# Loads of q, k and v on two queues, and a new order table, in a fused attention and maxout kernel

## The chip, the cores and the metric

The kernel runs on one core of a Trainium2 chip. The metric is the device time of one execution in microseconds (us). The kernel before has a median of 292.42 us over three timed runs (290.92 to 293.25).

## The reference

There are 64 heads (8 batches of 8), each with 576 tokens of 64 features, and a linear attention with exponential features, followed by a feed-forward layer with a maximum over three products:

```python
def phi(x):
    proj = np.einsum('bhsd,df->bhsf', x, w_phi)                # 64 -> 128
    proj = proj - np.max(np.abs(proj), axis=-1, keepdims=True)
    return np.concatenate([np.exp(proj), np.exp(-proj)], axis=-1)
q_p, k_p = phi(q), phi(k)
kv = np.einsum('bhsf,bhsd->bhfd', k_p, v);  z = np.sum(k_p, axis=2)
num = np.einsum('bhsf,bhfd->bhsd', q_p, kv)
den = np.einsum('bhsf,bhf->bhs', q_p, z)[..., None] + 1e-06
x = (num / den).transpose(0, 2, 1, 3).reshape(4608, 512)
h = np.maximum(np.maximum(x @ w1, x @ w2), x @ w3)             # 512 -> 768
return h @ w_out                                               # 768 -> 512
```

Inputs and output are float32. The kernel rounds to bfloat16 for its products.

## The kernel before

The work is cut into 16 units of four heads each, two units to a batch, and nine chunks of 512 tokens for the feed-forward layer. The Python code does not issue instructions where it describes them. It makes nodes: each node is a step on one engine, with the function that issues its instructions, the steps it depends on, and the buffers it touches. A table, `PLAN`, written out as text, then says in which order all 1479 nodes are issued, on which engine each one runs, and which slot of its pool each buffer takes. A word such as `1081G@5.1` is node 1081 on GpSimd (`G`; `D` VectorE, `A` ScalarE, `T` TensorE, `S` Sync) at a planned 5.1 us; digits behind the letter are the slots. Each engine executes its own words strictly in that order, and so do the queues from which DMAs are issued. The planned times only sort the words and, on TensorE, tell `fill` where fill products (`idler`) go in: products with no use that keep TensorE active in gaps of the first part.

A unit goes through these steps. The letters are the names of the node kinds, and the numbers are those of the units (K0 is the step K of unit 0).

- Loads of q, k and v. Units 0 to 3 have q and k transposed by TensorE, the others by a DMA transpose. Unit 0's q and k come in halves through Sync in float32 and are cast on chip (step C); those of units 1 to 3 come through GpSimd's queue, which casts to bfloat16 on the way. From unit 4 on, q and k come through Sync in float32 and GpSimd casts them. All v loads come through Sync. A one-element copy (gate) holds some v loads back.
- T, the transposition into qkT, and Tc, the copy out of PSUM.
- G, the products with w_phi (psq, psk); r, the maxima on VectorE; ek, the exponentials of k on ScalarE.
- E, the exponentials of the maxima (em), and va, the products of v with em into vab. These run on GpSimd. vd copies em beside them.
- M and eq, the features of q with their maxima taken off.
- K, the products of features and v: 72 small matmuls into kvps at L633, which need vab of the unit. kv copies them out.
- N and x, the numerator and the division; X, the transposition of the result into xT.

The weights w1, w2, w3 and w_out come through GpSimd's queue in four loads (W0, W1, W2 and wout), with a cast. The kernel uses max(a, b, c) = a + max(0, b - a, c - a): the differences w2 - w1 and w3 - w1 are formed on chip in three parts each (step wd, L775), the first three on GpSimd and the others on VectorE, and w1 is folded into w_out. For that, w1 is transposed on TensorE (wt at L787, into pwT, which needs W0) and multiplied with w_out (wm at L801, which needs wout). A chunk then is `up` and `up2` (L704), which need the differences, and `down` (L732, L737).

Of the kernel before, what the change touches and what calls it, by code (L numbers as in the profile page):

```python
# [19 lines left out]
P = 128  # L20
# [28 lines left out]
VA_DVE = 1  # L49
# [50 lines left out]
56A@14.3 35D@13.4 50A0@14.8 65A@15.0 104T111211@13.5 66T5@13.8 158G2@3.4 68A@15.5 108D@14.0 30D@14.6 46A@15.8 88T6@14.1  # L100
89D@15.2 92T7@14.9 93D@15.8 107D@16.0 60T3@15.3 61A@16.1 94T46@16.0 98D@16.6 105A@16.6 67A@17.1 99T71@16.8 102D@17.2
96A@17.4 62A@17.9 97D@17.9 101A@18.4 157G@4.2 163T5@17.6 164D2@18.5 1081G@5.1 1091T7@18.1 1092D0@19.1 109T34@18.7 112D@20.2
161T0@19.0 1084G@5.9 106A@18.9 110A@19.4 95A@19.9 1095T5@19.6 1096A@20.3 114T2@20.0 117D@20.8 116A@21.3 103D@21.2 162D@21.8
111A@21.7 1093T7@20.4 52G0@15.2 47G@16.3 115A@22.1 53G@17.4 49G@17.7 51G@18.0 48G@19.1 69T063@21.0 71A@22.5 133T51@22.1
134A@22.9 70A@23.4 130T0@22.6 159D2@22.4 113D@22.5 118D@23.1 1094D@23.5 100A@23.8 135A@24.3 230G0@20.2 1082G@21.0 229G@21.8
74T30@23.0 75D0@24.6 1083G@22.7 119A1@24.8 122G1@25.1 132A@25.0 78T4@23.4 127T2@23.7 136T6@24.1 137A@25.5 72T1@24.6
73D1@25.2 79D0@25.8 182T007500@25.0 185D@26.5 184A@26.0 138A@26.5 123A@26.9 186D@27.1 1099T3@25.4 1100D@27.7 1101T1@26.7
1102D@28.3 131A@27.2 129A@27.7 177T46@28.1 87S@7.4 120G@25.4 121G@26.5 172T70@28.3 175D@28.9 76T3@28.6 183A@28.2 128A@28.7
165T5@28.9 166D@29.5 178A@29.1 173A@29.6 179A@30.1 139T1@29.1 174A@30.6 1103T2@29.3 140A@31.1 1104A@31.4 180D@29.7 77D1@30.3
181D@31.0 187T7@30.6 191D@31.6 126G@27.7 125G@27.9 124G@29.1 142T154@30.9 176D@31.9 144A@32.1 141A@32.5 143A@32.9 367S1@17.2  # L110
370G1@30.2 167T36@31.9 171D@32.5 195A0@33.3 169A@33.5 189A@34.0 198A0@34.4 188A@34.5 1085G@31.3 235T2@32.3 236D0@33.1
170D@33.7 82T0@32.9 80T4@33.1 81A@34.9 145T11@33.4 146D0@34.3 147T5@33.8 148D1@35.0 190D@35.6 1097T2@34.1 168A@35.5 83A@36.0
1098A@36.6 149T3@35.4 150D0@35.9 151T1@35.7 152D1@36.5 233T4@36.0 234D@37.2 254T115711@36.6 256A@37.1 237T6@37.0 238D@37.8
257D@38.0 153T3@37.1 192T0@37.4 193A0@37.7 231D3@38.6 154A@37.9 155T2@37.5 156A@38.6 255A@39.2 160S@22.6 197G@33.7
244T14@37.9 247D@38.7 196G@35.8 214T006@38.2 216A@39.7 215D@39.4 245A@40.1 249T35@39.2 250A@40.6 252D@39.8 239T21@39.5
242D@40.4 240A@41.1 251A@41.6 258D@41.0 1090D@41.6 241A@42.1 1107T0@39.9 366S1@27.2 259T6@40.8 263D@42.2 1087G@37.9
1115T3@41.0 1116A1@42.5 1108A@43.0 261A@43.5 246A@43.9 1109T2@41.9 253D@42.5 369G@40.0 1088D@43.1 1117T7@42.7 1118A@44.4
302S0@32.6 305G2@41.1 194S@38.1 199T30@43.6 211T5@43.8 212A@44.9 213A@45.4 200A@45.7 243D@43.8 262D@44.4 248D@44.7
1129T0@43.9 1130D@45.3 1086G@42.2 1111T1@44.8 208T7@45.6 1112D@45.9 1110D@46.5 209A@46.2 267A1@46.7 264T4@45.9 265A1@46.9
1127T5@45.9 1128D@47.1 1113T0@46.8 202T1@47.7 432S1@38.8 435G0@44.3 232S@39.4 268G1@47.1 260A@47.2 210A@47.5 201A@48.0  # L120
1114A@48.5 205T2@47.9 207A@49.0 371S1@41.2 203A@49.5 204A@50.1 1089D@47.8 206A@50.6 372T004600@48.2 376D@48.6 387T57@48.4
389A@51.1 390D@49.2 375D@49.8 1119T3@48.7 1120D@50.4 301S0@44.1 1125T0@49.6 1126D@51.1 373A@51.6 270G@49.2 1121T5@50.5
388A@52.1 377T41@51.4 380D@51.9 1122D@52.5 382T32@51.7 385D@53.1 374A@52.5 1123T0@52.0 1124D@53.7 378A@53.0 1135T4@52.8
219T60@53.7 392T5@54.0 384A@53.5 379A@54.0 394A@54.5 266S@47.3 368S1@48.0 277T31@54.2 278A@54.8 692S0@48.6 431S1@49.3
283T0@54.5 285A@55.3 383A@55.7 304G@49.6 562S1@49.9 306S2@50.8 561S0@55.9 393A@56.2 284A@56.5 1136T@54.6 1137A0@56.8
1138S@57.6 220D0@54.3 381D@54.9 391D@55.5 386D@56.3 217T6@55.9 218D1@56.9 274T1@56.2 275A@57.4 395D@57.5 396D@58.0 276A@58.1
400A0@58.6 279A@58.8 1131T7@56.4 221T0@57.3 222D0@58.4 269G@50.7 286T124@57.7 288D@59.0 280T6@58.8 281A@59.3 223T5@59.0
397T1@59.3 398D0@59.6 287D@59.8 271T0@59.4 273A@59.8 282A@60.3 272A@60.8 402G0@59.0 434G@61.1 564G1@62.2 565G@63.3
225T3@59.6 226D@60.2 224D1@60.6 1132T@59.9 1133A1@61.4 312T114111@61.3 315D@61.7 307T23@61.5 322T65@61.8 323A@62.2 325D@62.3
293T01@62.1 294D0@62.9 310D@63.6 314A@62.7 324A@63.2 313A@63.7 316D@64.3 1139T7@62.4 326D@64.9 227T4@63.3 228D@65.5  # L130
399S@59.9 404T60@63.5 406A@64.1 309A@64.6 405A@65.1 1140T@63.8 327T0@65.1 328A@65.6 563S0@60.6 407T2@65.3 410T1@65.5
412A@65.9 1141A2@66.4 409A@67.0 311D@66.0 330D@66.6 295T5@65.7 411A@67.5 408A@68.0 331D@67.1 296D1@67.4 291T6@66.0
292D0@68.0 1143T4@66.3 289T7@67.2 290D1@68.6 436S0@62.3 303S2@65.2 496S1@65.8 329A@68.5 498S3@66.5 1144T@67.5 1145D3@69.3
308A@68.8 416T1@68.8 418A@69.3 413T5@68.9 415A@69.7 299T2@69.1 300A@70.2 297T6@69.4 298D@69.9 417A@70.8 317T07@69.8
320D@70.4 321D@71.0 695G2@64.4 403G@65.5 401G@65.8 419T034@70.0 421D@71.6 499G0@71.6 332T6@71.2 333D1@72.0 334S@72.3
335A1@71.7 338G1@72.7 337G@73.0 420D@72.2 1155T2@71.2 1167T0@72.1 1156D0@72.6 1168D@73.3 319A@72.0 414A@72.5 318A@73.0
447T001400@73.1 449A@73.5 452T63@73.3 455D@73.9 453A@74.0 437T52@73.5 439A@74.5 448A@75.0 438A@75.5 454A@75.9 440D@74.5
450D@75.1 441D@76.1 1157T7@73.9 1158A@76.4 1165T0@74.7 457T6@75.6 459A@76.9 428T50@75.8 429D0@76.7 566S1@73.0 628S1@75.9
451D@77.3 461D@77.9 1153T1@76.1 1154A@77.3 1166D@78.3 1149T2@77.0 442T75@77.9 443A@78.4 445D@78.9 1150A@78.9 458A@79.4
444A@79.7 336G@75.1 354T114@78.2 356A@80.2 355D@79.5 424T0@79.3 348T21@79.6 349A@80.6 460D@79.9 425D1@80.2 350A@81.2  # L140
# [145 lines left out]
def kernel(  # L286
# [133 lines left out]
    def attention(u):  # L420
# [4 lines left out]
        def nd(kind, *args, **kw):  # L425
            return node(kind, u, *args, **kw)
# [437 lines left out]
```

## Time and profile before

| what | value |
|---|---|
| timed runs | 290.92, 292.42, 293.25 us |
| span of the profiled execution (its own time; the profile gives no other for it) | 290.5 us |
| median of the runs less that span | 1.92 us |
| TensorE busy | 276.3 us (95%) |
| VectorE, ScalarE, GpSimd busy | 213.8, 193.8, 116.9 us |
| read from HBM, written to it | 34.67 MB, 9.44 MB |

The profile is of one execution. Its page gives, for each engine, the time in which it was busy, and the same in 40 equal slices as digits (9 is 90% or more). The engines are called PE (TensorE; PEld are its weight loads), DVE (VectorE), ACT (ScalarE), POOL (GpSimd) and SP (Sync); a q behind the name is the engine's issuing queue. PEclk is the clock that TensorE was granted, in tenths of full speed. The chain is the path of work that ended last, followed back from the end. In rows of a group, the numbers behind the first bar are the busy time in us and the mean of one in ns; behind the second bar stands how long the engine was idle ahead of them, and what ended that. In a timeline, a row begins with its start and length in us; brackets hold the idle time ahead and its releaser. For DMA issues, the last number is the time from issue to landing in us.

### The profile page before, as it was taken

The page shows a single profiled execution, that of the slowest core. Times are in us where ns is not written, and L with a number is a line of the kernel's source. Part 1 is how long each engine was busy: PE and PEld are TensorE (multiplying, and loading weights), DVE is VectorE, ACT ScalarE, POOL GpSimd, SP SyncE. Part 2 cuts the span into 40 slices and gives each one's busy share as a digit, 9 for nine tenths or more (in the row PEclk, how much of TensorE's full clock was granted, in tenths as well). Part 3 has the DMA queues.
Part 4 walks back from the last instruction along what each step waited for, and adds up shares of the span by engine and source line. Part 5 has one row for each costly group of instructions (what it writes and reads, how often), then busy time and mean ns, then how long its engine had stood idle before and what let it go on. Part 6 is the DMA issues. An engine that isn't in the chain of part 4 may idle for free.

```text
span 290.5 us, 8509 instructions
## 1 busy us (share of the span) xinstructions
PE 276.3 (95%) x3518; PEld 157.4 (54%) x3555; DVE 213.8 (74%) x449; ACT 193.8 (67%) x446; POOL 116.9 (40%) x99
## 2 busy tenths in 40 slices
PE   8678999899999999999999999999999999999995
PEld 3447676356656655555555566555544654444443
DVE  5695899998998967988979879878963382455411
ACT  1795989789898989976797898858758510021021
POOL 8055789728373662817180753500077001000000
PEclk9997999999999999999999999999999999999999
DMA  7999967899999999997999545982240109414045
GB/s 184 280 242 199 246 198 181 197 360 212 231 241 361 150 257 253 275 262 157 225 324 273 118 83 156 164 167 45 52 115 2 39 10 208 91 39 95 12 122 170
DMA packets 65649, 50.83 MB, mean 175 GB/s; under 512 B 46154, under 2 KB 50378, under 8 KB 65610
## 3 DMA queue, kind: packets, MB, share of 16 engines
q1 hardware_dynamic: 61279, 45.03, 63.2%
q0 software_dynamic: 4000, 4.92, 9.9%
q8 instruction: 28, 0.46, 0.6%
q10 hardware_dynamic: 331, 0.33, 0.3%
q14 instruction: 11, 0.09, 0.1%
HBM read 34.67 MB, written 9.44 MB: 152 GB/s over the span
## 4 chain that ended last, share of the span: by engine, by line
PE 66%; DMA 13%; DVE 10%; POOL 5%; issue 2%; SPq 2%; ACT 2%; ACTq 0%; POOLq 0%; DVEq 0%
PE ups L704 22%; PE ops L737 13%; PE ops L732 9%; DMA w_bf<-in_moe_w_dram 6%; PE psn L651 5%; DMA qkT<-qk_bf 5%; PE kvps L633 5%; PE psm L604 3%; PE psq L525 3%; DVE mk L544 3%; DVE hT L710 2%; POOL vab L579 2%; DMA q_raw<-in_q_dram 2%; DVE mqp L544 2%; PE pm L801 2%
## 5 line engine op out<-in xcount | busy, mean ns | idle before, releaser
L704 PE MATMUL ups<-xT,w_bf 128*128 128x512 bf16 x412 | 101.7, 379 | 2.5 <-DVE mk L544 0.9
L617 ACT ACTIVATE Eq<-psm 128x512 bf16<-128x512 f32 (+1 forms) x160 | 82.3, 584 | 9.6 <-PE psm L604 8.2
L579 POOL TENSOR_TENSOR vab<-v_raw,em 128x1152 bf16<-128x1152 f32 (+1 forms) x36 | 67.9, 1904 | 44.6 <-ACT em L575 31.7
L538 ACT ACTIVATE Ek<-psk 128x512 bf16<-128x512 f32 x128 | 70.6, 616 | 8.3 <-PE psk L525 5.1
L704 PEld LDWEIGHTS <-w_bf 128*128 128x128 bf16 x432 | 40.6, 98 | 47.2 <-issue 2.3
L544 DVE TENSOR_REDUCE mqp<-psq 128x4 bf16<-128x512 f32 (+1 forms) x80 | 48.8, 632 | 8.3 <-PE psk L525 4.9
L737 PE MATMUL ops<-wout_bf,hT 128*128 128x512 bf16 (+1 forms) x215 | 50.4, 373 | 0.4
L710 DVE TENSOR_TENSOR hT<-hT,ups 128x512 bf16<-128x512 bf16 x54 | 35.9, 681 | 12.3 <-PE ups L704 8.5
L544 DVE TENSOR_REDUCE mk<-psk 128x4 f32<-128x512 f32 x64 | 42.6, 682 | 1.8 <-PE psk L525 1.1
L745 ACT COPY osb<-ops 128x512 f32<-128x512 f32 (+1 forms) x18 | 10.5, 590 | 38.2 <-PE ops L737 35.7
L737 PEld LDWEIGHTS <-hT 128*128 128x128 bf16 x222 | 21.0, 98 | 22.3
L658 DVE TENSOR_TENSOR x_sb<-psn,rden 128x320 bf16<-128x320 f32 x64 | 31.5, 491 | 2.2
L712 ACT ACTIVATE hT<-ups 128x512 bf16<-128x512 f32 x32 | 19.8, 627 | 17.2 <-PE ups L704 17.2
L651 PEld LDWEIGHTS <-Eq 128*128 128x128 bf16 x640 | 25.2, 97 | 7.7
L651 PE MATMUL psn<-kv_sb,Eq 128*128 128x65 bf16 x640 | 27.3, 194 | 0.0
L745 DVE COPY osb<-ops 128x512 f32<-128x512 f32 (+1 forms) x19 | 12.8, 673 | 19.5 <-PE ops L737 16.4
L732 PE MATMUL ops<-xT 128*128 128x512 bf16 x89 | 24.0, 380 | 0.4
L525 PE MATMUL psq<-w,qkT 64*128 64x128 bf16 x256 | 21.5, 219 | 0.8 <-DMA qkT<-qk_bf 0.8
L604 PE MATMUL psm<-qkT,wphi_m 128*128 128x512 bf16 (+1 forms) x70 | 22.3, 358 | 0.0
L525 PE MATMUL psk<-w,qkT 64*128 64x128 bf16 x256 | 21.4, 219 | 0.0
L714 DVE TENSOR_SCALAR hT<-ups 128x512 bf16<-128x512 f32 x22 | 14.8, 685 | 8.4 <-PE ups L704 8.4
L633 PE MATMUL kvps<-vab,Ek 64*128 64x65 bf16 x1152 | 20.1, 190 | 0.4 <-POOL vab L579 0.4
(76 smaller groups left out, 266.7 us busy)
## 6 DMA issues: line engine op xcount, KB each, us to landing
v_raw<-in_v_dram SPq DMA_DIRECT2D x16, 576.0 KB, 5.4
out_dram<-osb SPq DMA_DIRECT2D x66, 128.0 KB, 2.4
k_raw<-in_k_dram SPq DMA_DIRECT2D x12, 576.0 KB, 4.5
q_raw<-in_q_dram SPq DMA_DIRECT2D x12, 576.0 KB, 6.0
w_bf<-in_moe_w_dram POOLq DMA_DIRECT2D x3, 768.0 KB, 17.0
qk_bf<-in_q_dram POOLq DMA_DIRECT2D x3, 288.0 KB, 10.9
qk_bf<-in_k_dram POOLq DMA_DIRECT2D x3, 288.0 KB, 10.7
wout_bf<-in_moe_w_out_dram POOLq DMA_DIRECT2D x1, 768.0 KB, 21.0
```

Source lines behind the costliest of these rows:

```text
L525: nc.tensor.matmul(ps()[:, i, :], lhsT=cols[r, :], rhs=w2[r, c, :], start=True, stop=True)
L538: nc.scalar.activation(Ek[s]()[:, tiles_of(t0, n), :], of(1), EXP, scale=1.0 - 2.0 * s)
L544: nc.vector.tensor_reduce((mq, mk)[c]()[:, tiles_of(t0, n)], of(c), AXX, ALU.max, apply_absolute_value=True)
L579: (nc.vector if n_.eng == "DVE" else nc.gpsimd).tensor_tensor(vab()[:, g, t0:t1, 0:D], vb()[:, t0:t1, :], em()[:, g, t0:t1].unsqueeze(2).t ...
L617: nc.scalar.activation(Eqb()[s][:, cols], psm()[:, 0:w], EXP, scale=1.0 - 2.0 * s)
L633: nc.tensor.matmul(kvps[ab]()[:, t // NT, g, :], lhsT=Ek[g]()[r, t, :], rhs=vab()[r, g, t, :], start=(t + g == 0), stop=(t == UT - 1 and g ...
L651: nc.tensor.matmul(psn()[:, c, :], lhsT=Eqb()[g][:, t0:t0 + P], rhs=kv()[:, pr, ab, g, :], start=(g == 0), stop=(g == 1))
L658: nc.vector.tensor_tensor(x_sb()[:, pr, :, ab, :], psn()[:, :, 0:D], rden().to_broadcast([P, 5, D]), ALU.mult)
L704: nc.tensor.matmul(ups(), lhsT=w_bf[i + 1][:, ct, j * P:(j + 1) * P], rhs=tokens_of(ct), start=(ct == 0), stop=(ct == CT - 1))
L710: nc.vector.tensor_tensor(hT()[:, j, :], hT()[:, j, :], ups(), ALU.max)
L732: nc.tensor.matmul(ops_()[:, 0:width], lhsT=tile_of(ct, tt), rhs=line_w[c_i > MOVE][:, ct, cols], start=(ct == 0), stop=False)
L737: nc.tensor.matmul(ops_()[:, 0:width], lhsT=hT()[:, j, tt * P:(tt + 1) * P], rhs=wout_bf[:, j, cols], start=False, stop=(j == JT - 1))
```

## The change

- `VA_DVE` goes. The products of v may run on VectorE for unit 0, at a new planned cost; the table still has them all on GpSimd.
- q, k and v loads in float32 (all but unit 0's q and k) may be issued by Sync or by GpSimd. The table puts 12 q and k loads and 3 v loads on GpSimd: v of units 0, 2 and 9, and q or k of units 4, 5, 7, 8, 10, 11, 12, 13, 14 and 15. Sync keeps the others.
- Unit 0's q and k lie side by side in qk_bf, so that one 128-column transpose turns both, where a 64-column transpose each did. That is 18 transposes instead of 36. The casts into qk_bf run on ScalarE, all four; two of them were on VectorE.
- All six weight differences run on GpSimd. Three were on VectorE.
- `PLAN` is another table: order, engines, slots and planned times. The DMA order on GpSimd becomes k1, q1, W0, k2, q2, v0, wout, W1, k5, q5, k3, q3, v2, W2, k4 and so on; it was q1, k1, k2, q2, W0, wout, k3, W1, q3, W2. Sync starts with q0, k0, k0, q0 in halves, and then v1. Six kv copies and two copies out of wm go from VectorE to ScalarE, six of the chunks' rectifications from ScalarE to VectorE, three stores from Sync to ScalarE. There are 26 fill products instead of 23. The amount of other TensorE work is the same.

```diff
-VA_DVE = 1
 ...
 PLAN = (another table)
 ...
-    queue_of = {"SP": nc.sync, "ACT": nc.scalar}
+    queue_of = {"SP": nc.sync, "ACT": nc.scalar, "POOL": nc.gpsimd}
 ...
-        qk = buf("qk_bf", QK, [P, 2, UT, D] if by_pe else [P, UT, 2 * D], BF16)
+        qk = buf("qk_bf", QK, [P, 2, UT, D] if by_pe and u else [P, UT, 2 * D], BF16)
 ...
-                            copy_on[n_.eng](qk()[:, what, ts, :], raw()[:, ts, :])
+                            copy_on[n_.eng](qk()[:, ts, what * D:(what + 1) * D], raw()[:, ts, :])
 ...
-                mains.append(nd("Lv" if what == 2 else "L", {"SP": 0.62}, lambda what=what, raw=raw: nc.sync.dma_start(
-                    by_pairs(raw()), rows_of(what, u, 0, 2)), gates, [raw],
 ...
+                n_ = nd("Lv" if what == 2 else "L", {"SP": 0.62, "POOL": 0.75}, None, gates, [raw],
 ...
+                n_.fn = lambda n_=n_, what=what, raw=raw: queue_of[n_.eng].dma_start(by_pairs(raw()), rows_of(what, u, 0, 2))
+                mains.append(n_)
 ...
+                        if u == 0:
+                            nc.tensor.transpose(tps()[:, n, :], qk()[:, t, :], ident)
+                            continue
                         for c in range(2):
                             nc.tensor.transpose(tps()[c * D:(c + 1) * D, n, :], qk()[:, c, t, :], ident)
 ...
-                if VA_DVE > u:
-                    costs["DVE"] = 0.11 + 0.105 * (t1 - t0)
+                if u == 0:
+                    costs["DVE"] = 0.11 + 0.064 * (t1 - t0)
 ...
-            n_ = node("wd", 0, {"DVE": 0.6} if i else {"POOL": 2.1}, None, [w_nodes[0], w_nodes[i + 1]], [])
+            n_ = node("wd", 0, {"DVE": 1.2, "POOL": 2.1}, None, [w_nodes[0], w_nodes[i + 1]], [])
```

More of the change, by code (lines that the diff above doesn't have):

```diff
@@ L100 @@
[L100 to L109, printed above, removed]
@@ L462, in attention @@
                         raw()[0:1, 0, 0:1], src()[0:1, col:col + 1]), [], [src, raw]))
-                mains.append(nd("Lv" if what == 2 else "L", {"SP": 0.62}, lambda what=what, raw=raw: nc.sync.dma_start(
-                    by_pairs(raw()), rows_of(what, u, 0, 2)), gates, [raw],
-                    pipe=(EARLY if u == 0 or u == BY_PE and what == 1 else 1.0) * FULL, hold=-3.0, lat=1.7,
-                    packet=PACKET))
+                n_ = nd("Lv" if what == 2 else "L", {"SP": 0.62, "POOL": 0.75}, None, gates, [raw],
+                        pipe=(EARLY if u == 0 or u == BY_PE and what == 1 else 1.0) * FULL, hold=-3.0, lat=1.7,
+                        packet=PACKET)
+                n_.fn = lambda n_=n_, what=what, raw=raw: queue_of[n_.eng].dma_start(by_pairs(raw()), rows_of(what, u, 0, 2))
+                mains.append(n_)
         for c in range(0 if by_pe else 2):
```

280 lines of the change are left out of this document (148 added, 132 removed).

## The prediction

> **What bounds the kernel now.** I read the page first: the span, the busy shares, the slices and the chain.
>
> ```profile
> span 290.5 us, 8509 instructions
> PE 276.3 (95%) x3518; PEld 157.4 (54%) x3555; DVE 213.8 (74%) x449; ACT 193.8 (67%) x446; POOL 116.9 (40%) x99
> ...
> PE   8678999899999999999999999999999999999995
> ...
> PEclk9997999999999999999999999999999999999999
> DMA  7999967899999999997999545982240109414045
> ...
> PE 66%; DMA 13%; DVE 10%; POOL 5%; issue 2%; SPq 2%; ACT 2%; ACTq 0%; POOLq 0%; DVEq 0%
> ```
>
> TensorE is busy in nine tenths of every slice but the first four and the last, and carries two thirds of the chain. Only the first 29 us, where PE has holes and one slice of reduced clock, have much to give. So I cut the span at PE's landmarks: its longest hole, the first key-value product (unit 0's kvps, K0), and the fifth (unit 5's, K5).
>
> ```profile
> core 0: us, PE busy (x) PEld busy (x) DVE busy (x) ACT busy (x) POOL busy (x), PEclk, DMA share, GB/s
> 20.54:22.98 2.44, 0.00 (x1) 0.00 (x1) 1.03 (x2) 1.34 (x3) 2.44 (x3) 0.96 1.22 207
> 22.98:27.01 4.03, 4.03 (x50) 3.34 (x51) 1.64 (x3) 1.64 (x3) 2.45 (x4) 0.60 1.19 195
> 27.01:78.04 51.03, 49.42 (x828) 31.26 (x835) 48.09 (x103) 46.48 (x113) 35.12 (x26) 1.00 0.93 229
> 78.04:290.50 212.46, 206.02 (x2440) 113.97 (x2464) 148.72 (x307) 131.60 (x302) 68.24 (x50) 1.00 0.66 155
> ```
>
> PE stands for 2.44 us, then works 4.03 us at a clock of 0.60. From K0 on it idles 1.61 us in 51.03, and 6.44 us in the last 212.46. The timeline tells who ended the hole, and the chain in order of time what was on the path:
>
> ```profile
> 22.98 1.03 PE L787 MATMUL pwT<-ident,w_bf 128*128 128x128 bf16 x8 [2.44 <-DMA w_bf<-in_moe_w_dram]
> 27.01 1.27 PE L633 MATMUL kvps<-vab,Ek 64*128 64x65 bf16 x72
> 78.04 1.26 PE L633 MATMUL kvps<-vab,Ek 64*128 64x65 bf16 x72
> ```
> ```profile
> 4.96 17.97 DMA w_bf<-in_moe_w_dram
> ...
> 48.04 0.88 DVE w_bf L775
> ...
> 49.85 1.53 DVE w_bf L775
> ...
> 55.37 1.56 DVE w_bf L775
> ...
> 287.07 0.37 ACT osb L745
> ```
>
> W0 (the first maxout weight) is issued at 4.96 and lands at 22.93; its transposes on PE wait for it with everything behind them. Later, three weight differences on VectorE (3.97 us) lie on the chain.
>
> **The change, part by part.** *The waypoint.* In the two orders the same PE instructions stand ahead of K5, apart from fill products and unit 0's transposes, and so the same ones behind it. Ahead of K0 the new order has everything that the old one has, and four transposes of unit 2 and three M groups of unit 1 more. So the gain is K0's shift, plus the work that is now ahead of K0, plus what changes in the holes after K0.
>
> *GpSimd's DMA queue.* Old: q1, k1, k2, q2, W0, wout. New: k1, q1, W0, k2, q2, v0, wout, W1, k5, q5, k3, q3 (a letter and its unit). W0 moves past two loads, and v0 comes from Sync to sixth place here. The rates, from the old queue:
>
> ```profile
> 2.82 1.46 POOL L452 DMA_DIRECT2D qk_bf<-in_k_dram  x2
> ...
> 4.25 0.75 POOL L452 DMA_DIRECT2D qk_bf<-in_q_dram  x1
> ...
> 5.71 0.88 POOL L413 DMA_DIRECT2D wout_bf<-in_moe_w_out_dram  x1
> ...
> 9.60 0.67 ACT L445 CAST qk_bf<-q_raw 128x576 bf16<-128x576 f32 x1 [1.08 <-DMA q_raw<-in_q_dram]
> ...
> 22.44 0.77 POOL L452 DMA_DIRECT2D qk_bf<-in_k_dram  x1
> ```
> ```profile
> DMA to landing us min/median/max: 5.8/10.8/14.9
> ```
> ```profile
> qk_bf<-in_k_dram POOLq DMA_DIRECT2D x3, 288.0 KB, 10.7
> wout_bf<-in_moe_w_out_dram POOLq DMA_DIRECT2D x1, 768.0 KB, 21.0
> ```
>
> The middle answer is that of the qk_bf tile. k1, issued at 2.82, landed 10.7 us later, at 13.5; q2 (4.25 + 14.9) at 19.2; W0 at 22.9; wout (5.71 + 21.0) at 26.7; k3 (22.44 + 5.8) at 28.2. So a weight takes 3.8 us of the queue, a q or k load 1.5 us when no Sync load runs beside it, and 2.8 us each ((19.2 - 13.5) / 2) with Sync loads beside it. In the new order Sync has its four halves in by 9.6, as now, and then only v1, which waits behind some ten VectorE instructions for a gate that comes at about 16 (estimate). From 9.6: k1 needs half a load more, 10.3; q1 11.8; W0 15.6; k2 17.1; q2, v0 and v1 share three loads' time, 21.6. Not shown before is a GpSimd load without a cast; I take the read bytes, which are the same. Bounds for v0: 20.1 without v1, and 27.4 if every q, k and v load from 9.6 on takes 2.8 (9.6 + 5 x 2.8 + 3.8). I take 21.6, since the 2.8 had three Sync loads beside three.
>
> *K0.* K0 needs unit 0's four products with v on GpSimd, which are now behind v0's landing:
>
> ```profile
> 17.72 2.26 POOL L579 TENSOR_TENSOR vab<-v_raw,em 128x576 bf16<-128x576 f32 x2 [11.14 <-ACT em L575]
> ...
> 20.23 2.26 POOL L579 TENSOR_TENSOR vab<-v_raw,em 128x576 bf16<-128x576 f32 x2
> ```
>
> Two take 2.26, four 4.5: 21.6 + 4.5 = 26.1, and K0 at 26.2 instead of 27.01: 0.8 gained. (24.7 and 32.0 at the bounds.) Of the old 6.5 us of hole and slow clock only this comes back, because the wait goes from W0 to q2 (PE's transposes of unit 2, about 1.7 us late) and then to v0. A second slow-clock stretch there would be hidden under the wait for v0.
>
> *Work ahead of K0.* The three M groups and four transposes move into the time in which PE waits anyway:
>
> ```profile
> 17.60 0.30 PE L483 MATMUL tps<-ident,qk_bf 128*64 128x128 bf16 x4
> ...
> 28.21 0.39 PE L606 MATMUL psm<-qkT,w 128*128 128x512 bf16 x1
> ...
> 28.67 0.38 PE L606 MATMUL psm<-qkT,w 128*128 128x512 bf16 x1
> ```
>
> One M group is 28.67 - 28.21 = 0.46, with a shorter third one and 0.3 for the transposes: 1.4 us. If K0 were not held by v0, this would be worth nothing; at the low bound of v0 I still count it.
>
> *Weight differences.* All six now on GpSimd.
>
> ```profile
> L579 POOL TENSOR_TENSOR vab<-v_raw,em 128x1152 bf16<-128x1152 f32 x28 | 58.9, 2121 | 33.5 <-ACT em L575 20.5 <-issue 10.6 <-DMA v_raw<-in_v_dram 2.4
> L469 POOL CAST qk_bf<-k_raw 128x1152 bf16<-128x1152 f32 x12 | 14.1, 1182 | 15.1 <-DMA k_raw<-in_k_dram 11.4 <-DMA qkT<-qk_bf 3.7
> ...
> L775 POOL TENSOR_TENSOR w_bf<-w_bf 128x1024 bf16<-128x1024 bf16 x3 | 6.8, 2269 | 0.0
> ```
>
> VectorE loses 3.97 us in a stretch where it sets the pace; GpSimd gains three of 2.27. PE's holes from K0 to K5 sum to 1.61, so no more than 1.6 can come back; I take 1.0. GpSimd becomes tight: from 26.1 stand v1's four products (4.5), three differences (6.8), two casts (2.3), three more differences (6.8), two casts (2.3), the products of units 2 and 3 (four of 2.12, 8.5) and three DMA issues (2.3): 33.5 us, to 59.6. PE, with 51.0 us between K0 and K5 and unit 3's product (K3) about two thirds of the way by the instructions between, comes to K3 at about 26 + 0.67 x 49 = 59. So this is even; each us more on GpSimd there is one on PE. Bounds: +1.6 to -2.
>
> *Issues and waits.* Fifteen q, k, v loads go to GpSimd at 0.75 each; only three lie in the tight stretch (counted). The ninth DMA of that queue waits for the first one's landing, and so on: k5, q5, k3, q3 wait for k1, q1, W0, k2 (17.1), and the products of unit 0 stand behind them; all are in before v0, so this costs nothing as long as v0 comes later than k2.
>
> One rule speaks against moving loads: the Trainium skill, DMA: Bandwidth & Descriptors, section SWDGE vs HWDGE vs iDMA, says that GpSimd writes descriptors into SBUF through a port that VectorE can lock, which Sync's issues never touch. The longest GpSimd issue here is this one:
>
> ```profile
> 1.89 0.94 POOL L452 DMA_DIRECT2D qk_bf<-in_q_dram  x1
> ```
>
> With 0.94 for each, three issues in the tight stretch would cost 0.6 us more, and the sum would end at 289.8; the 0.75 at 4.25 and the 0.77 at 22.44 do not show it.
>
> *Moves between VectorE and ScalarE.* Six copies of kv and two of the folded weights go to ScalarE, six rectifications come to VectorE.
>
> ```profile
> L714 DVE TENSOR_SCALAR hT<-ups 128x512 bf16<-128x512 f32 x22 | 14.8, 685 | 8.4 <-PE ups L704 8.4
> ...
> L638 DVE CAST kv_sb<-kvps 128x260 bf16<-128x260 f32 x17 | 7.1, 421 | 4.6 <-PE kvps L633 4.5
> ```
>
> 6 x 0.685 - 6 x 0.421 is 1.6 us more for VectorE over the whole span, in which it is 26% idle: nothing.
>
> *The casts of unit 0 and its full-width transposes.* ScalarE's 0.67 for VectorE's 0.75 and 0.52: nothing, since the second half's cast waits for 9.6 as before; 18 transposes for 36: nothing for the same reason. Without that cover it would be a few tenths either way.
>
> *After K5.* The same PE work in another order. Of PE's 6.44 us of holes some 3 lie after its last matmul (the copy at 287.07 waits for it), so an order can gain or lose about 3.3. I take 0.
>
> *Sum.* 0.8 + 1.4 + 1.0 = 3.2 us; span 290.5 - 3.2 = 287.3. The median of the timed runs, 292.42, is 1.92 above the profiled span: 289.2.
>
> **The rivals.** *First, slower: v0 late.* The GpSimd queue passes at the company rate, v0 lands at 27.4, K0 runs at 32.0. That is 5.0 lost, 1.4 back, and GpSimd's tight 33.5 us moves with it: 292.42 + 3.6 = 296.0. For it: a queue of twelve, one after another. Against: Sync is nearly empty then. It decides from v0 at 24.8, where the gain is gone; 1% slower from about 27.7, or from 26 with GpSimd's stretch 2 us longer.
>
> ```profile
> 24.65 0.79 POOL L413 DMA_DIRECT2D w_bf<-in_moe_w_dram  x1
> ```
>
> *Second, taken back later.* After 80 us, POOL's loads and Sync's DMA transposes share the 16 engines, which were hardly together before: the last load of GpSimd's ten was issued at 24.65. If they hold PE by the 3.3 us above, the front's gain is gone: 292.5. For it: DMA slices at 9 up to the middle. Against: in one queue a transpose already stands behind the load in front of it.
>
> *Third, the hole only moves.* W0 comes early, but PE waits as long in front of unit 2's transposes, the slow clock falls behind K0 (0.4 of 4.03, 1.6 us) and GpSimd's differences take back the 1.0: 0.8 + 1.4 - 1.6 = 0.6, 291.8. For it: one 2.44 us hole was enough for a stretch at 0.60. That stretch agrees with the Trainium skill, TensorE: Matmul & The Clock Gate, Part 1, in kind, though its idle window is about 3.4 us.
>
> **How the numbers follow.** About 1% (289.5 and 295.3) is what the timed runs can tell from no change. The forecast, a gain of 2 to 6: 0.50, of which 0.42 under 289.5. First rival 0.22, of which 0.20 over 295.3. Second 0.14, third 0.14, nearly all within 1%, with 0.02 under 289.5 where the later order gains instead. Faster 0.44, same 0.36, slower 0.20. Range: low, v0 at 20.1 (2.3) + 1.4 + 1.6 and 1.6 of the 3.3 later: 6.9, so 285.5; high, near the first rival, 295.5.
>
> **What would show it.** PE's wait in front of pwT is gone; v0's products begin on GpSimd near 21.6; K0 near 26.2; K5 at 74.8 instead of 78.0; 212 us from there to the end; no w_bf on VectorE. The prediction is wrong if K0 is later than 29, if K5 to the end takes over 214, or if GpSimd ends the waits of K2 and K3.

## The result, and the profile after

The changed kernel takes 288.15 us (median of four runs, 287.0 to 289.06) against 291.98 for the kernel before beside it (290.92 to 293.25). The ratio is 0.9875 with a 95% interval of 0.983 to 0.992: 1.2% faster. A second set of six runs gave 287.62, ratio 0.9854 (0.9817 to 0.9891). The profiled execution took 289.06 us, of which 287.3 is its span.

The page of the changed kernel, with the lines that answer to those of before:

```profile
span 287.3 us, 8483 instructions
PE 276.2 (96%) x3501; PEld 157.3 (55%) x3540; DVE 209.5 (73%) x441; ACT 192.4 (67%) x449; POOL 133.1 (46%) x119
...
PE   8989999999999799999999999999999999999994
...
PEclk9999999999999889999999999999999999999999
...
PE 89%; ACT 4%; DVE 3%; DMA 2%; issue 1%
```

PE's busy time is what it was (276.2 for 276.3), and GpSimd has 16 us more work. The holes of the first slices and the slice of reduced clock there are gone. A hole and two slices of reduced clock now stand near 100 us. DMA went from 13% of the chain to 2%.

The windows between the same landmarks: K0 is at 23.32 instead of 27.01, K5 at 72.73 instead of 78.04. The last two rows are the new hole and the slow stretch behind it. Columns: the stretch, its length, busy time of each engine, granted clock, DMA share, GB/s.

```profile
0.00:23.32 23.32, 20.99 (x267) 12.60 (x268) 16.90 (x44) 17.39 (x40) 14.63 (x24) 1.00 1.03 226
23.32:72.73 49.41, 48.08 (x804) 30.26 (x811) 44.53 (x98) 44.42 (x108) 44.83 (x36) 1.00 1.09 279
72.73:287.30 214.57, 207.11 (x2439) 114.41 (x2464) 148.11 (x301) 130.57 (x304) 73.63 (x61) 0.99 0.66 148
95.75:97.70 1.95, 0.00 (x1) 0.00 (x0) 0.40 (x1) 1.95 (x6) 0.00 (x0) 1.00 0.39 106
98.58:101.99 3.41, 3.41 (x12) 1.34 (x11) 1.55 (x3) 0.63 (x2) 0.00 (x0) 0.50 1.38 270
```

Ahead of K0, PE idles 23.32 - 20.99 = 2.33 us; before it idled 6.15 (27.01 less the 20.86 busy that the 276.3 leave there). The busy time there is about the same (20.99 for 20.86) although more work is done, since none of it runs at the half clock. So 3.7 us are won by K0 and 5.3 by K5, and 2.1 are lost again behind K5 (214.57 for 212.46).

The timeline shows where the wait went. First GpSimd's and Sync's queues, then PE:

```profile
3.53 0.79 POOL L418 DMA_DIRECT2D w_bf<-in_moe_w_dram  x1
...
5.68 0.78 POOL L471 DMA_DIRECT2D v_raw<-in_v_dram  x1
...
19.19 4.48 POOL L588 TENSOR_TENSOR vab<-v_raw,em 128x576 bf16<-128x576 f32 x4 [0.17 <-DMA v_raw<-in_v_dram]
```
```profile
14.59 0.39 SPq L471 DMA_DIRECT2D v_raw<-in_v_dram  x1
```
```profile
17.01 0.61 PE L796 MATMUL pwT<-ident,w_bf 128*128 128x128 bf16 x8
19.45 0.30 PE L492 MATMUL tps<-ident,qk_bf 128*64 128x128 bf16 x4 [0.55 <-DVE qkT L495]
20.64 0.21 PE L534 MATMUL psk<-w,qkT 64*128 64x128 bf16 x1 [0.39 <-DVE mqp L553]
...
23.32 0.19 PE L642 MATMUL kvps<-vab,Ek 64*128 64x65 bf16 x1
```

Before, pwT had [2.44 <-DMA w_bf]; now PE never waits for a weight ahead of K0. In the trace W0 lands at 14.63 (11.10 after its issue), and its first transposes run at 15.7. v0 lands at 19.11, the products with it start at 19.19 and K0 follows at 23.32 behind only 0.55 and 0.39 us of holes.

### The profile page after: what moved, and what is told of

It reads as the page before. It is cut to its first block, busy times and chain, and to the rows that moved or that the text cites. A ratio compares the mean times of both kernels' runs of the same rounds, so it can differ in the third digit from the quotient of the medians.

```text
span 287.3 us, 8483 instructions
## 1 busy us (share of the span) xinstructions
PE 276.2 (96%) x3501; PEld 157.3 (55%) x3540; DVE 209.5 (73%) x441; ACT 192.4 (67%) x449; POOL 133.1 (46%) x119
## 4 chain that ended last, share of the span: by engine, by line
PE 89%; ACT 4%; DVE 3%; DMA 2%; issue 1%
PE ups L713 32%; PE ops L746 16%; PE ops L741 10%; PE psn L660 7%; PE kvps L642 6%; PE psm L613 5%; PE psq L534 5%; PE idler L841 3%; DMA qkT<-mT 2%; PE pm L810 2%; ACT Ek L547 2%; ACT Eq L626 2%; PE psq L529 1%; DVE mk L553 1%; DVE mqp L553 1%
## 5 line engine op out<-in xcount | busy, mean ns | idle before, releaser
L626 ACT ACTIVATE Eq<-psm 128x512 bf16<-128x512 f32 (+1 forms) x160 | 81.0, 596 | 8.9 <-PE psm L613 8.6
L547 ACT ACTIVATE Ek<-psk 128x512 bf16<-128x512 f32 x128 | 73.5, 624 | 7.5 <-DVE mk L553 3.5
L746 PE MATMUL ops<-wout_bf,hT 128*128 128x512 bf16 (+1 forms) x214 | 51.9, 381 | 0.5 <-issue 0.2
L746 PEld LDWEIGHTS <-hT 128*128 128x128 bf16 x222 | 21.6, 99 | 23.9 <-issue 1.6
L660 PEld LDWEIGHTS <-Eq 128*128 128x128 bf16 x640 | 26.2, 98 | 11.5 <-issue 2.5
L660 PE MATMUL psn<-kv_sb,Eq 128*128 128x65 bf16 x640 | 28.3, 194 | 2.0 <-ACT Ek L547 2.0
L721 ACT ACTIVATE hT<-ups 128x512 bf16<-128x512 f32 x26 | 15.9, 622 | 19.9 <-PE ups L713 19.9
L723 DVE TENSOR_SCALAR hT<-ups 128x512 bf16<-128x512 f32 x28 | 18.9, 686 | 11.9 <-PE ups L713 11.7
L754 DVE COPY osb<-ops 128x512 f32<-128x512 f32 (+1 forms) x18 | 12.0, 674 | 20.0 <-PE ops L746 17.4
```

The source lines that it names most:

```text
L547: nc.scalar.activation(Ek[s]()[:, tiles_of(t0, n), :], of(1), EXP, scale=1.0 - 2.0 * s)
L626: nc.scalar.activation(Eqb()[s][:, cols], psm()[:, 0:w], EXP, scale=1.0 - 2.0 * s)
L660: nc.tensor.matmul(psn()[:, c, :], lhsT=Eqb()[g][:, t0:t0 + P], rhs=kv()[:, pr, ab, g, :], start=(g == 0), stop=(g == 1))
L746: nc.tensor.matmul(ops_()[:, 0:width], lhsT=hT()[:, j, tt * P:(tt + 1) * P], rhs=wout_bf[:, j, cols], start=False, stop=(j == JT - 1))
```

## The experiments

Parts of the change were taken out of the new kernel one by one, and two were put into the old one. Words of `PLAN` are given as in the code. K0, K5 and the time from K5 to the end are those of each profile, which is of one execution; each ratio is to the kernel before as timed beside it (medians from 291.55 to 292.17).

| kernel | time, median | ratio to before (95%) | K0 | K5 | K5 to end |
|---|---|---|---|---|---|
| before | 291.98 | 1 | 27.01 | 78.04 | 212.5 |
| changed | 288.15 | 0.9875 (0.983 to 0.992) | 23.32 | 72.73 | 214.6 |
| changed, second set | 287.62 | 0.9854 (0.9817 to 0.9891) | 23.42 | 72.34 | 212.6 |
| old early DMA order | 294.96 | 1.0087 (1.0048 to 1.0126) | 31.61 | 81.11 | 212.0 |
| W0 fifth | 289.36 | 0.993 (0.9905 to 0.9954) | 27.04 | 76.75 | 211.9 |
| 15 loads on Sync | 296.17 | 1.013 (1.0069 to 1.0192) | 32.95 | 80.80 | 212.5 |
| v0 alone on Sync | 288.1 | 0.9873 (0.9833 to 0.9914) | 24.46 | 73.93 | 211.9 |
| 12 later loads on Sync | 287.2 | 0.9842 (0.9805 to 0.988) | 22.94 | 75.62 | 211.7 |
| 11 later loads on Sync | 286.57 | 0.982 (0.9788 to 0.9852) | 23.47 | 72.67 | 211.3 |
| differences on VectorE | 289.34 | 0.9893 (0.984 to 0.9946) | 23.94 | 75.10 | 213.0 |
| half-width transposes | 286.46 | 0.9801 (0.9762 to 0.984) | 24.01 | 72.78 | 211.9 |
| half-width and 11 loads | 285.5 | 0.9795 (0.9757 to 0.9833) | 23.40 | 71.58 | 210.8 |
| before, W0 third | 292.28 | 1.0024 (0.9995 to 1.0054) | 27.73 | 78.76 | 211.4 |
| before, differences on GpSimd | 295.7 | 1.0106 (1.0077 to 1.0136) | 26.28 | 81.24 | 215.8 |

### The early order of the loads, taken back

```diff
-1081G@3.3        14G0@5.5   367G1@7.7
+1081G@4.75       14S0@3.2   367S1@7.7      (W0 fifth; v0 and k5 on Sync)
```

> The changed kernel with the early DMA order as it was: v0 and k5 issued by Sync, W0 fifth on GpSimd's queue. Theory F (the gain is made ahead of K0 by the early DMA order): W0 lands at 20 to 23 instead of 14.6, TensorE waits 2 us or more in front of the pwT transposes, K0 runs at 26 to 27.5 instead of 23.3, and the time is 2 to 3.5 us over the changed kernel's. Theory W (the gain comes from the weight differences that left VectorE) and theory O (from the order of everything behind K0): K0 may be late, but the time stays within 1 us of the changed kernel's.

Measured: 294.96 us, 6.8 more than the changed kernel and 3.0 more than the kernel before. The timeline and the window up to K0:

```profile
22.44 1.03 PE L796 MATMUL pwT<-ident,w_bf 128*128 128x128 bf16 x8 [5.36 <-DMA w_bf<-in_moe_w_dram]
```
```profile
0.00:31.61 31.61, 22.40 (x267) 13.48 (x268) 17.61 (x44) 17.73 (x41) 13.80 (x23) 0.89 1.05 236
```

W0 lands at 22.40, hardly earlier than in the kernel before (22.93), but PE now waits 5.36 us for it instead of 2.44: in the new order pwT stands earlier on PE, with less work ahead of it. A stretch of 6.83 us at half clock begins inside this hole, at 19.43. From K0 on nothing is lost: 49.50 to K5 and 212.0 from there. Theory F holds in kind, but its sizes were too small: K0 comes at 31.61 instead of 26 to 27.5, and 6.8 us are lost instead of 2 to 3.5. Without the early loads nothing of the gain is left, and the new order of PE is then slower than the old one. This isn't the old order of the loads in every word: W1 stays ahead of k3, and q5 and v2 stay on GpSimd.

### W0 alone put back to fifth place

```diff
-1081G@3.3
+1081G@4.75
```

> The changed kernel with W0 fifth on GpSimd's queue, behind k2 and q2, v0 still sixth. Theory F in its narrow form (W0's place alone makes the gain): K0 back near 26, time 2 us or more over the changed kernel's. Theory F in its wide form (the whole queue and an empty Sync): W0 lands at about 17.6 (14.6 and two loads of 1.5), TensorE stands about 2 us in front of pwT, but K0 waits for v0's products until 23.7 anyway, so K0 moves by 1 us at most and the time by 0 to 1 us. Theories W and O: no difference.

Measured: 289.36 us. W0 lands at 18.00, and PE waits:

```profile
18.05 0.62 PE L796 MATMUL pwT<-ident,w_bf 128*128 128x128 bf16 x8 [2.22 <-DMA w_bf<-in_moe_w_dram]
```

A stretch of 3.41 us at half clock follows, and K0 is at 27.04, as late as before the change. In this profile all that the early loads had won by K0 is gone with this one word. The median is only 1.2 to 1.7 us above the changed kernel. The profiled execution took 290.37 and is one of five with a clock of 0.993 or 0.994, which took 290.2 on the mean. Four others showed 0.999 and took 289.2; a stretch of 3.41 us at half clock would have taken 0.006 off that mean, so they had none. K0 came even later than the narrow form of theory F had it (near 26), and the time lies between the two forms. The wide form had the wait in front of pwT right (2 us), but not the half clock behind it.

### All fifteen loads back on Sync

```diff
-14G0@5.5 367G1@7.7 366G1@8.4 160G@23.9 302G0@36.4 562G0@58.6 ... 822G1@141.0
+14S0@5.5 367S1@7.7 366S1@8.4 160S@23.9 302S0@36.4 562S0@58.6 ... 822S1@141.0
```

> The changed kernel with all fifteen float32 loads of q, k and v that GpSimd issues issued by Sync at the same places of the table. Theory F: v0, k5 and q5 run beside GpSimd's queue and take 1.8 MB of its share before W0 and q2 are in, so W0 lands at 18 to 19 and q2 at 21 to 22, K0 runs at 25 to 26, and the time is 1.5 to 3 us over the changed kernel's. The rival (queue choice is free, only the order counts): K0 and the time within 1 us. The second rival of the prediction (loads on GpSimd beside DMA transposes cost something later): K5 to the end shortens by 1 us or more against the changed kernel's 214.6.

Measured: 296.17 us, the slowest of the variants of the changed kernel. Two long holes stand ahead of K0:

```profile
19.68 0.62 PE L796 MATMUL pwT<-ident,w_bf 128*128 128x128 bf16 x8 [2.91 <-DMA w_bf<-in_moe_w_dram]
```
```profile
25.79 0.95 PE L492 MATMUL tps<-ident,qk_bf 128*64 128x128 bf16 x14 [3.82 <-DMA qk_bf<-in_q_dram]
```

W0 is third in GpSimd's queue here too, but Sync issues v0, k5 and q5 at 2.76, 3.23 and 3.85 beside it. W0 lands at 19.64 instead of 14.63, and q2 at 25.75 instead of 17.62. So it is not the place in the queue alone: what Sync loads beside it counts too. Theory F had the direction, but W0 at 18 to 19, q2 at 21 to 22 and a loss of 1.5 to 3 us; the loss is 8. From K5 to the end it takes 212.5, against 212.6 to 214.6 with the loads on GpSimd, so those loads cost little or nothing there.

### Only v0 back on Sync, and only the twelve later loads

```diff
-14G0@5.5
+14S0@3.2
```

> The changed kernel with one DMA different: unit 0's v load goes to Sync again (behind the four halves of unit 0's q and k), the other fourteen stay on GpSimd. If each load that Sync has beside GpSimd's queue delays that queue by one load's time and no more: v0 lands near 13, W0 near 16.1 instead of 14.63, k2 and q2 near 17.5 and 19.1, the products with v0 run while PE has other work, K0 between 22.5 and 24.5, time 287.5 to 289.5. If company on Sync slows the GpSimd queue to the old 2.8 us a load: W0 after 18, K0 near 27 as with W0 fifth, time 289.5 to 291.

Measured: 288.1 us, ratio 0.9873, as the changed kernel. W0 landed at 15.62, k2 at 17.80, q2 at 19.11, K0 at 24.46. Against the first profile of the changed kernel, W0, k2 and q2 are 1.0 to 1.7 us later; against the second, 0.5 to 1.5. That is about one load's time, as the first expectation had it. K0 comes 1.0 to 1.1 later, in this execution without a stretch at half clock. Two of the other five had a clock of 0.988 and took 289.94 and 292.63, so the loss isn't always that small. The 8 us above are not v0's by itself; whether k5 and q5 make them, or only all three together, no run tells apart.

```diff
-160G@23.9 302G0@36.4 562G0@58.6 ... 822G1@141.0
+160S@23.9 302S0@36.4 562S0@58.6 ... 822S1@141.0
```

> The changed kernel with the twelve q, k and v loads issued after 23 us back on Sync; v0, k5 and q5, the three early ones, stay on GpSimd. If only the early loads matter: K0 23.3 and K5 72.7 as in the changed kernel, 212 to 214.6 from K5 to the end, time within 1 us of the changed kernel, 287 to 289. If the later loads on Sync stand in the way of its DMA transposes: holes in front of qkT's readers after 40 us, time 290 or more.

Measured: 287.2 us, the same as the changed kernel. The twelve later loads are worth nothing on GpSimd; the three early ones (v0, k5, q5) are all that differs between this kernel and the one with fifteen on Sync, so the 9 us between those two are theirs. From K5 to the end: 211.7. The profiled execution took 289.11, nearly 2 us more than the median, and K5 is at 75.62, not at the expected 72.7. It had this:

```profile
28.82 1.22 PE L810 MATMUL pm<-wout_bf,hT 128*128 128x512 bf16 x4 [2.17 <-DMA wout_bf<-in_moe_w_out_dram]
```

wout landed at 28.78 instead of 24.29. Sync moved v1, v2 and k4 beside it, where the changed kernel has v1 alone. A stretch of 3.41 us at half clock followed at 29.52. So v2 was put back on GpSimd and the eleven after it left on Sync:

```diff
-302G0@36.4 562G0@58.6 ... 822G1@141.0      (160G@23.9 stays)
+302S0@36.4 562S0@58.6 ... 822S1@141.0
```

> As the kernel with the twelve later loads on Sync, but unit 2's v load, the first of the twelve, stays on GpSimd. With all twelve on Sync, wout landed at 28.78 instead of 24.29 in the profile, since that v load ran beside it, and PE stood 2.17 us at 28.82. If that is the cause: wout lands near 24.3, no hole near 28.8, no half clock at 29.5, profiled span 284.3 to 285.5, median 286.2 to 287.2, the fastest of all. If the hole was chance: the same median within 0.3 of the kernel with twelve, 286.9 to 287.5, with or without a hole there.

Measured: 286.57 us, ratio 0.982. wout landed at 26.41, not near 24.3 as expected, since Sync still moved k4 and v1 beside it; the hole is gone. In these profiles wout lands at 24.29 to 24.80 with one load of Sync beside it, at 25.70 and 26.41 with two, and at 28.78 with three. But all five other executions of the kernel with twelve showed a clock of 0.999 or 1.0, so none of them had a stretch at half clock. The loss belongs to that one execution; the two medians differ by less than the runs spread, and whether v2's queue matters for the time stays open.

### The weight differences, in both orders

```diff
-1088G@41.3 1090G@45.5 1089G@47.6
+1088D@41.3 1090D@45.5 1089D@47.6
```

> The changed kernel with the three differences of the third weight on VectorE again, at the same places of the table. Theory W: VectorE pays 3 x 1.4 us where it sets the pace, K5 runs 2 to 4 us later than 72.7, and the time is 2 to 3 us over the changed kernel's. Theory F: GpSimd gets 6.3 us free, VectorE has room in the new order, K5 within 1 us of 72.7 and the time within 1 us.

Measured: 289.34 us, 1.2 and 1.7 above the two sets of the changed kernel. The intervals of the ratios overlap, so that a loss is likely and not shown. The window from K0 to K5, and the longest hole in it:

```profile
23.94:75.10 51.16, 48.61 (x805) 30.55 (x812) 47.10 (x101) 44.44 (x108) 38.28 (x33) 1.00 1.01 269
```
```profile
45.49 0.21 PE L534 MATMUL psq<-w,qkT 64*128 64x128 bf16 x1 [0.77 <-DVE mk L553]
```

PE idles 2.55 us there instead of 1.33 (0.61 in the second profile of the changed kernel), and the longest of these holes is behind VectorE. K5 is 2.4 us later than in the first profile, of which 0.6 arose ahead of K0. So theory W had the place right and the time too large (2 to 3 us); theory F had both too small. The opposite test, in the kernel before:

```diff
-1090D@41.6 1088D@43.1 1089D@47.8
+1090G@41.6 1088G@43.1 1089G@47.8
 ...
-            n_ = node("wd", 0, {"DVE": 0.6} if i else {"POOL": 2.1}, None, [w_nodes[0], w_nodes[i + 1]], [])
+            n_ = node("wd", 0, {"DVE": 0.6, "POOL": 2.1}, None, [w_nodes[0], w_nodes[i + 1]], [])
```

> The kernel before with one part of the change: the three weight differences that VectorE made go to GpSimd; DMAs and the other engines' orders stay. If they cost PE time in the old order by holding VectorE (the chain of before shows 3.97 us of them): the holes between K0 and K5 go from 1.61 to 0.6 or less, time 0.8 to 1.6 less than the kernel before, 290.3 to 291.1. If the gain of 1.2 that the changed kernel has of it belongs to the new order, in which everything comes 4 us earlier: within 0.6 of the kernel before, 291.3 to 292.5. If GpSimd becomes late for unit 3's and 4's products instead: holes in front of kvps after 60 us, 292.5 or more.

Measured: 295.7 us, 1.1% slower than the kernel before. GpSimd's and PE's timelines:

```profile
57.00 2.13 POOL L775 TENSOR_TENSOR w_bf<-w_bf 128x1024 bf16<-128x1024 bf16 x1
```
```profile
51.87 0.82 PE L704 MATMUL ups<-xT,w_bf 128*128 128x512 bf16 x3 [1.05 <-POOL w_bf L775]
59.18 1.04 PE L704 MATMUL ups<-xT,w_bf 128*128 128x512 bf16 x4 [2.33 <-POOL w_bf L775]
```

The last difference ends at 59.1, and the first `up` steps wait for it. In the changed kernel the six run earlier, with W1 at 28.10 instead of 32.56 and another order on GpSimd:

```profile
L784 POOL TENSOR_TENSOR w_bf<-w_bf x6: 2110/2120/2138, 29.8 to 47.3; 128x1024 bf16<-128x1024 bf16 x6
```

(The profiled execution took 298.84 us, 3 more than the median, so the rows show the place of the loss and not its size.) The expected gain and the expected "no change" both missed. The third expectation had the time (292.5 or more) and the late engine, GpSimd, but another place: these holes are in front of `up`, not of kvps. The same move costs 3.1 (by the ratio) to 3.5 us (by the medians) in the old order. In the new one it does not cost, and likely gains 0.5 to 1.7.

### W0 early in the old order

```diff
-1081G@5.1
+1081G@3.0
```

> The kernel before with one DMA moved: the first maxout weight goes third instead of fifth in GpSimd's queue, ahead of unit 2's k and q; PE's order and all else as before. If the early weight is worth something only with the new order on PE (in the old order unit 2's transposes stand ahead of the weight's): W0 lands near 16, q2 near 22.9, PE stands at unit 2's transposes near 22.9 instead of at the weight's, K0 within 1 us of 27.0, time 290.5 to 293, the same as before. If the early weight is the gain in itself: K0 23.5 to 25, time 287.5 to 289.5.

Measured: 292.28 us, ratio 1.0024 (0.9995 to 1.0054), no change. The timeline and the windows around the wait:

```profile
22.46 1.07 PE L483 MATMUL tps<-ident,qk_bf 128*64 128x128 bf16 x16 [3.70 <-DMA qk_bf<-in_q_dram]
```
```profile
0.00:22.46 22.46, 16.64 (x192) 8.65 (x192) 14.87 (x37) 14.08 (x31) 11.80 (x21) 0.95 1.02 236
22.46:27.73 5.27, 5.27 (x67) 4.34 (x68) 2.33 (x5) 1.78 (x3) 1.79 (x3) 0.56 1.21 208
```

W0 lands at 19.27 (v0, v1 and a k load of Sync beside it; I had expected 16) and q2 at 22.42. In the old order unit 2's transposes stand ahead of pwT, so PE waits for q2 until 22.46, nearly as long as it waited for W0 (22.98). The hole only moved. This run moves W0 alone: v0 stays on Sync, and W0 doesn't get as early as in the changed kernel (14.63). The whole early order of the loads, with v0 and k5 off Sync, was not run under the old order of PE.

### Unit 0's transposes in half width again

```diff
-[P, 2, UT, D] if by_pe and u else [P, UT, 2 * D]
+[P, 2, UT, D] if by_pe else [P, UT, 2 * D]
 ...
-                            copy_on[n_.eng](qk()[:, ts, what * D:(what + 1) * D], raw()[:, ts, :])
+                            copy_on[n_.eng](qk()[:, what, ts, :], raw()[:, ts, :])
 ...
-                        if u == 0:
-                            nc.tensor.transpose(tps()[:, n, :], qk()[:, t, :], ident)
-                            continue
 ...
-                       [qk, tps], mode=2 * (u > 0))
+                       [qk, tps], mode=2)
```

> The changed kernel with unit 0's transposes in the old half-width form (two per tile, 36 instead of 18, the casts into separate halves of qk_bf); DMAs, order and engines stay. If the full-width tiles are worth nothing, as I costed them, because PE waits for unit 0's second halves and later for v0's products anyway: first products K0 at 23.3 to 23.7, time within 0.7 of the changed kernel, 287 to 288.6. If they are worth their PE time (18 transposes at some 0.06 us, 1.1 us): K0 near 24.4, time 288.5 to 289.5.

Measured: 286.46 us, ratio 0.9801. The full-width tiles are worth nothing in the time, as costed. K0 is 0.6 to 0.7 later (24.01), between the two expectations, and K5 in the same place (72.78); with half-width transposes and eleven loads on Sync, below, K0 is at 23.40. A time below the changed kernel's stood in neither expectation. It isn't shown either, since the intervals of the ratios overlap; the next two tests bear on it.

### The changed kernel again: is the hole at 97.70 part of it?

The kernel is the same. In the first profile of the changed kernel, the row behind the hole is this:

```profile
97.70 0.47 PE L660 MATMUL psn<-kv_sb,Eq 128*128 128x65 bf16 x10 [1.95 <-ACT Ek L547]
```

> The changed kernel once more, for its number and for its hole of 1.95 us at 95.75. If that hole comes of the order (PE waits for something that is late each time): it is there again, between 1.5 and 2.4 us, at the same psn instruction near 97.7, with a stretch of half clock behind it, and the time is 287.5 to 289. If it is a delay that differs from run to run: it is somewhere else, or under 1 us, with no half clock near 100, and K5 to the end takes 211.5 to 213.5. The time is 287 to 289 either way, 0.983 to 0.992 of the kernel before.

Measured: 287.62 us. The second profile has, at the same instruction and from K5 to the end:

```profile
96.98 0.47 PE L660 MATMUL psn<-kv_sb,Eq 128*128 128x65 bf16 x10 [0.90 <-ACT Eq L626]
```
```profile
72.34:284.90 212.56, 207.37 (x2470) 113.89 (x2464) 148.28 (x301) 130.71 (x304) 74.05 (x61) 1.00 0.67 149
```

The hole is there again at the place that the first expectation gave. In length (under 1 us), clock and time from K5 to the end it is as the second had it: 212.56, as before the change (212.46). So the 2.1 us lost in the first profile are not a fixed cost of the order. What holds PE there isn't settled. In the first trace ScalarE's copy of kv, which psn needs, had ended at 95.54, 2.2 us before PE went on. In both traces two instruction loads by DMA meet there, within 0.25 us of each other, and one of the two takes 2.04 us (from 94.33; mostly 0.9 to 1.2) and 1.79 us (from 93.70; mostly 0.3 to 0.5). With half-width transposes, which shift PE's instructions, they are 4 us apart, take 0.35 and 1.06 us, and there is no hole. That would fit a PE that lacks its next instructions. But with v0 on Sync two loads met as well (1.76 us from 94.44) and PE had no hole there, while with the differences on VectorE they were 3.3 us apart and PE idled 0.79 us (at 98.52), one instruction further on. No run took the meeting away alone, so it stays open.

The other traces add something. In all five full-width kernels with W0 fifth or with one, eleven, twelve or fifteen loads on Sync, a hole of 0.95 to 1.31 us stands some 6 to 7 us behind this place. It waits for a DMA; this is the one with v0 on Sync:

```profile
104.25 0.39 PE L613 MATMUL psm<-qkT,wphi_m 128*128 128x512 bf16 x1 [0.95 <-DMA qkT<-mT]
```

The two half-width traces have neither hole.

### The two variants together

The half-width transposes and the eleven later loads on Sync, both edits as above:

```diff
+[P, 2, UT, D] if by_pe else [P, UT, 2 * D]
 ...
+302S0@36.4 562S0@58.6 ... 822S1@141.0
```

> The two last variants together: the changed kernel with unit 0's transposes in the half-width form and the eleven latest q, k and v loads on Sync (v0, k5, q5 and v2 stay on GpSimd). If each of the two takes away a delay of its own, they add: ratio to the kernel before 0.974 to 0.979, time 284.5 to 286. If both only leave out the hole near 97.7 that the changed kernel had in its two profiles (1.95 and 0.90 us), they do not add: ratio 0.979 to 0.983, time 286 to 287.2, K0 near 24, K5 near 72.8, 211 to 212 from there to the end and no hole over 1.2 us after K5.

Measured: 285.5 us (284.16 to 286.83), ratio 0.9795 (0.9757 to 0.9833). The page's first line and the windows:

```profile
span 282.4 us, 8516 instructions
```
```profile
0.00:23.40 23.40, 20.95 (x285) 12.48 (x286) 16.94 (x44) 17.39 (x40) 14.81 (x24) 1.00 1.04 235
23.40:71.58 48.18, 47.48 (x803) 30.05 (x811) 44.33 (x98) 44.30 (x108) 41.05 (x31) 1.00 1.07 279
71.58:282.40 210.82, 205.44 (x2439) 113.89 (x2464) 148.14 (x301) 130.66 (x304) 69.34 (x55) 1.00 0.67 151
```

It beats the kernel before by 2.0% and has the lowest ratio of all, though not one that can be told from that of the half-width variant. Its interval just overlaps that of the changed kernel (0.9817 to 0.9891), so the 0.6 to 0.8% between the two are likely and not shown. The ratio is about that of the half-width variant alone (0.9801) and lies in the range of the second expectation, by which the two parts don't add and both leave out the hole near 97. But K5 (71.58 instead of near 72.8), K5 to the end (210.8) and the time (285.5) are all below what that expectation named, and the time lies in the range of the first. Neither is settled. PE has no hole over 0.55 us in this trace up to its last matmul, so the hole near 102 of the kernel with eleven loads on Sync (1.04 us) is gone as well.

## Why the prediction was right, point by point

The total (289.2) was within 1.1 of the first median and 1.6 of the second, and the direction and range held. The terms, against the two profiles of the changed kernel:

| term | forecast | first profile | second profile |
|---|---|---|---|
| K0 earlier | 0.8 | 3.7 | 3.6 |
| K0 to K5 shorter | 1.4 + 1.0 | 1.6 | 2.1 |
| K5 to the end longer | 0 | 2.1 | 0.1 |
| span | 287.3 | 287.3 | 284.9 |

The span of the first profile is exactly the forecast, and that is luck, by errors that met: K0 was undersized by 2.9, K0 to K5 was oversized by 0.8, and 2.1 were lost behind K5. The direction, and that early loads make the gain, were right; the reason given for the size of K0's shift was not.

*GpSimd's queue.* This is the mis-sized term. Forecast were landings of k1 10.3, q1 11.8, W0 15.6, k2 17.1 and v0 21.6; the trace has 9.42, 10.85, 14.63, 16.06 and 19.11 (the second profile 19.97 for v0). The rate of 1.5 us a load and 3.8 for W0 was right (1.43 to 1.56, and 3.78). Two things were not. k1 was through when Sync's halves were in, at 9.42 instead of 10.3. And v1, which I put beside q2 and v0 (three loads' time for two), was issued at 14.59, but its packets moved from 18.11 to 21.82, most of them beside wout: wout took 5.18 (24.29 less 19.11) and v0 only 1.49. That company, 1.4 us more than a weight's 3.78, belonged behind v0.

*"Of the old 6.5 us of hole and slow clock only this comes back."* Wrong for that reason. The wait did not go to q2 and then to v0: PE waits nowhere for q2 in the first profile and 0.41 us in the second. PE's idle time ahead of K0 fell by 3.8 us (2.8 in the second), and the half clock there is gone. The four products take 4.48 us (forecast 4.5) from v0's landing, but PE reaches K0 by its own work shortly before they end (23.32 and 23.67). So K0 is no longer the sum of v0 and the products, as the forecast had it; PE waits for them only inside K0. The row of the second profile:

```profile
24.59 0.69 PE L642 MATMUL kvps<-vab,Ek 64*128 64x65 bf16 x34 [0.33 <-POOL vab L588]
```

*Work ahead of K0.* Forecast 1.4 us less from K0 to K5: PE's busy time there went from 49.42 to 48.08, 1.34 less, and to 48.31, 1.11 less, in the second profile. Right.

*Weight differences.* Forecast 1.0, at most 1.6. PE's idle time between K0 and K5 went from 1.61 to 1.33 in the first profile and to 0.61 in the second; putting the three back on VectorE likely costs 0.5 to 1.7 us of time, which isn't clear of the spread. So 1.0 is within what can be told, and no more than that. That GpSimd would be "even" held: K3 came at 57.28 (forecast 59) and did not wait. What the text lacked is that this depends on the order around it: in the old order the same move costs 3.1 to 3.5 us. One reading in the prediction's opening was too coarse: PE's eighth slice in the page of before, from 50.8 us, is an 8 too, with a hole of 0.88 us at 51.32 in it.

*Issues.* k5, q5, k3 and q3 were issued at 9.70, 11.14, 15.20 and 16.35, each right behind the landing of k1, q1, W0 and k2, and were in time, as forecast. By the Trainium skill (DMA: Bandwidth & Descriptors, SWDGE vs HWDGE vs iDMA), VectorE can lock GpSimd out of the SBUF state in which it writes descriptors. The prediction priced that at 0.6. The issues ahead of K0 took 0.72 to 0.93 us, as before, and moving the twelve later loads between the queues changed nothing that can be measured (287.2 for 287.62). No run shows the rule to matter here.

*Full-width transposes and moves between VectorE and ScalarE.* Costed at nothing. For the first the runs bear it out (286.46 with half-width transposes, no slower); the second was not tested alone.

*After K5.* Forecast 0, and "wrong if over 214". The first profile has 214.57, which by that sentence speaks against me. The second has 212.56, and the nine variants of the changed kernel have 210.8 to 213.0, so 0 is right within the spread of the traces. The first profile is above them by its hole of 1.95 us and the stretch at half clock behind it; the hole itself is in the second profile too (0.90).

*The rivals.* The first (v0 late) fell: v0 landed at 19.1, not 27.4. With the fifteen loads back on Sync the time is its 296.0 (296.17), but by chance: there PE waits for W0 and q2, not for v0. The second (taken back by GpSimd's late loads) fell with the twelve loads on Sync: same time. The third (the hole only moves) is what one part of the change does by itself: W0 early in the old order moves the hole from pwT to unit 2's transposes, 3.70 us for 2.44, and the time stays.

## What to carry to other kernels

An in-order DMA queue and an in-order engine are one schedule: loads put in the order in which the engine uses them, with little beside them, came with a gain of 3.8 to 4.3 us here. The weight alone moved ahead under the old order of PE gained nothing, and the new order of PE under nearly the old loads was a loss of 3. Test parts of such a change in both directions, since a part can help in one order and hurt in the other (the weight differences: a loss of 3.1 to 3.5 us in the old order, a likely gain of 0.5 to 1.7 in the new). When a sum comes out exactly, compare its terms at the landmarks before believing it, and take a second profile where a term is off by more than the runs spread.

## What the runs showed of the hardware that was not expected

Holes shorter than the slow stretch can bring the whole of it. PE's holes of 1.95, 2.17, 2.22, 2.28, 2.33, 2.44 and 2.62 us each ended within 1.2 us of the start of a stretch at half clock of 3.41 us, and those of 3.70 us and more stood beside one of 6.83. Holes of up to 1.46 us never were, and one of 2.40 (at 10.32 in the kernel before) and one of 2.91 (at 19.68 with all loads on Sync) were not. A stretch of 3.41 us at half clock costs some 1.7 us where PE sets the pace (an estimate, half its length), so a hole of 2 us can cost nearly 4. In the kernel with W0 fifth, the executions with the stretch took 1.0 us longer on the mean than those without. The Trainium skill (TensorE: Matmul & The Clock Gate, Part 1) has the same 3413 ns as a window, free-running, but lets the clock drop after an idle window of about 3.4 us; no hole of 1.95 us can hold one, so a window need not be idle throughout. In the kernel before, the executions of all sets showed a granted clock of 0.987 to 0.998; in the second set of the changed kernel all six showed 0.999 or 1.0. So part of the gain is that clock.
